# Seven-product matmul for one more batch of a fused attention and MLP-mixer kernel, with three weight sums moved

## The chip, the cores and the metric

The kernel runs on one core of one Trainium2 chip. The metric is the device time of one execution in microseconds (us). PE is TensorE, PEld its weight loads, DVE VectorE, ACT ScalarE, POOL GpSimd, SP SyncE, which issues most of the DMAs.

## The reference

Eight batches of a linear attention with cosine weights (8 heads, 576 rows, head width 64) feed an MLP mixer: a token part, then a channel part of two matmuls (512 to 1536 to 512). Cut to what matters:

```python
q_p, k_p = phi(q), phi(k)              # relu, times cos and sin of the position
kv  = einsum('bhsf,bhsd->bhfd', k_p, v)
x   = einsum('bhsf,bhfd->bhsd', q_p, kv) / den     # 8 x 576 x 512 in all
h   = maximum(x.T @ w_tok1, 0) @ w_tok2
u   = x + h.T
h2  = maximum(u @ w_ch1, 0) @ w_ch2    # the second channel matmul
out = u + h2
```

## The kernel before

A batch has 576 rows: 512 are worked on as four tiles of 128 rows, and the last 64 of two batches share one tile. These tail tiles of all eight batches are kept (`u_tail`) and go through the channel part together at the very end, as a ninth pass.

Each batch passes through the same steps. `feat` makes q and k features on ACT or DVE (its last letter: A or D; P is POOL), `cast` turns v to bf16, `turnx` transposes q features by DMA from SP's queue into `qpT`. `kvm` and `kvo` form and copy kv. `numf` and `numfo` form the numerator and divide it on DVE. `mix` and `mixo` are the first token matmul with relu, `um` the second. `uo` (DVE) adds x, `ubc` (POOL) casts to bf16, `utx` transposes the result by DMA into `uT`. `up` and `upo` are the first channel matmul and its relu into `h1` (12 blocks of 128 channels by 512 rows). The second channel matmul has two forms. In the plain one, `dn` adds 12 matmuls of 128x512 for each of four row tiles (`dnw` and `dnj` are orders of it), and `o` adds u on DVE and stores. In the other, `channel7`, h1 and `w_ch2` are split in two by two blocks, and seven products of block sums (Winograd's form of Strassen's method) take the place of eight: each product is 12 matmuls of 128x256. `p1` to `p7` are the products with the sums that follow them, `s_part` and `s3` make sums of h1 blocks on DVE, and `quad_weights` makes sums of blocks of `w_ch2`: t1 (in place of one block), t2, t3 and t4.

All instructions are in an order written by hand, on each engine in program order. The string `PLAN` (lines 18 to 57) lists the first part word by word: all of batches 0 and 1 through their channel parts, the attention of batch 2 and the features of batch 3. Both batches use the plain form of the second channel matmul there. From line 837 a loop runs p = 2 to 7: `channel7` does the channel part of batch p (lines 664 to 736), and after each of its slots calls hooks (`hooks7`) that issue attention of batch p + 1, features of batch p + 2 and loads of p + 3. For p = 2 alone, hooks in slots 0 and 8 also issue the four weight sums. Each product of `channel7` shares one of four PSUM buffers (`psM`) with the first matmul's `c_ps`: p1 and p2 use one bank after the other, p5 and p3 too, so that ACT must have copied p1's result (`va`) before p2, and p5's (`vc`) before p3. p7's bank is the one that p2's sum frees. At the end `channel7` runs once more for the tail rows, with `fine=True`: other order of products, p4 in two halves, and stores after each part, from the queues of SP and ACT.

Of the kernel before, what the change touches and what calls it, by code (L numbers as in the profile page):

```python
# [9 lines left out]
F32 = mybir.dt.float32  # L10
# [5 lines left out]
QUADS = 2  # L16
# [29 lines left out]
cast.2.0.1.2.P kvm.2.2 kvo.2.2.A turnx.2.4.1 ld.3.k.2.wd6 o.0.3 up.1.0 upo.1.0.A up.1.9 numf.2.3 numfo.2.3  # L46
up.1.4 upo.1.9.A numf.2.1 up.1.2 numfo.2.1 upo.1.4.A o.0.1 up.1.5 numf.2.0 upo.1.5.A upo.1.2.A numfo.2.0
feat.3.q.3.2.0.A feat.3.q.1.2.0.A feat.3.q.2.2.0.D ld.3.v.2.v22 cast.3.4.1.2.P up.1.10 up.1.3 numf.2.2
mix.2.0.2 numfo.2.2 upo.1.10.D up.1.8 up.1.6 numf.2.4 feat.3.q.2.2.1.A upo.1.8.D mix.2.1.2 mix.2.2.2 up.1.1
numfo.2.4 feat.3.q.1.2.1.A mix.2.3.2 mix.2.4.2 mixo.2.2.A feat.3.q.3.2.1.D upo.1.3.D turnx.3.2.2  # L50
feat.3.q.4.2.1.D upo.1.1.D up.1.7 feat.3.q.0.2.0.A upo.1.6.A up.1.11 feat.3.k.2.2.0.D feat.3.q.4.2.0.D
feat.3.k.4.2.1.A turnx.3.4.1 feat.3.q.0.2.1.D upo.1.11.A um.2.1 um.2.0 feat.3.k.0.2.1.D upo.1.7.A
cast.3.1.1.2.P uo.2.1 ubc.2.1 uo.2.0 dnj.1.3.0 dnj.1.3.1 cast.3.3.1.2.D turnx.3.0.2 feat.3.k.0.2.0.A ubc.2.0
utx.2.1 dnj.1.0.0 utx.2.0 ld.4.q.2 dnj.1.2.0 tb.1 feat.3.k.4.2.0.A dnj.1.2.1 cast.3.0.1.2.D o.1.2
feat.3.k.1.2.0.A cast.3.2.1.2.P feat.3.k.2.2.1.D ld.4.v.2.k22 dnj.1.1.0 dnj.1.1.1 ld.4.k.2.k32 feat.3.k.3.2.1.A
dnj.1.0.1 feat.3.k.3.2.0.A feat.3.k.1.2.1.A o.1.0 o.1.3 tm.2 to.2 o.1.1
# [3 lines left out]
def kernel(  # L60
# [11 lines left out]
    nc = tc.nc  # L72
# [194 lines left out]
    def relu(eng, dst, src):  # L267
        if eng == "A":
            nc.scalar.activation(dst, src, AF.Relu)  # L269
        else:  # L270
            nc.vector.tensor_relu(dst, src)  # L271

    class Batch:
# [261 lines left out]

        def o(self, j):
            nc.vector.tensor_add(self.u[:, j, :], self.ps.pop(("o", j)), self.u[:, j, :])
            if j % 2:
                for p_ in range(2):
                    nc.sync.dma_start(out=out_rows(self.b, p_, j - 1, 2), in_=self.u[p_::2, j - 1:j + 1, :])  # L540
# [36 lines left out]
    def channel(uT, u, store, by_slot, hooks, fine=False):  # L577
        h1 = one.tile([P, NCH, 4 * P], BF16, name="h1")
        slot = 0
# [7 lines left out]
        for mi in range(NCH):  # L587
            c_ps = psM.tile([P, 512], F32, name="c_ps", tag="psM")
            for ki in range(NCC):
                nc.tensor.matmul(c_ps, wc1[:, ki, mi * P:(mi + 1) * P], uT[:, :, ki, :],  # L590
                                 start=(ki == 0), stop=(ki == NCC - 1))
            relu(by_slot[mi], h1[:, mi, :], c_ps)
            step()
        for j in range(4):
            if fine and j == 3:
                for cs in (slice(0, Dm // 2), slice(Dm // 2, Dm)):
                    o_ps = psM.tile([P, Dm // 2], F32, name="o_ps", tag="psM")
                    for ki in range(NCH):
                        nc.tensor.matmul(o_ps, h1[:, ki, j * P:(j + 1) * P], wc2[:, ki, cs],
                                         start=(ki == 0), stop=(ki == NCH - 1))  # L600
                    nc.vector.tensor_add(u[:, j, cs], o_ps, u[:, j, cs])
                    store(j, u, cs)
                break
            o_ps = psM.tile([P, Dm], F32, name="o_ps", tag="psM")
            for half in range(2):
                for ki in range(half * NCH // 2, (half + 1) * NCH // 2):
                    nc.tensor.matmul(o_ps, h1[:, ki, j * P:(j + 1) * P], wc2[:, ki, :],
                                     start=(ki == 0), stop=(ki == NCH - 1))
                if half:
                    nc.vector.tensor_add(u[:, j, :], o_ps, u[:, j, :])  # L610
                    store(j, u)
                step()

    K2, D2 = NCH // 2, Dm // 2
    t2, t3, t4 = (const.tile([P, K2, D2], BF16, name=f"t{i}") for i in (2, 3, 4))

    def quad(a, b):
        return wc2[:, a * K2:(a + 1) * K2, b * D2:(b + 1) * D2]

    t1 = quad(0, 1)  # L620

    def quad_weights():
        return [lambda: nc.vector.tensor_sub(t3, quad(1, 1), quad(0, 1)),
                lambda: nc.vector.tensor_sub(t1, quad(0, 1), quad(0, 0)),
                lambda: nc.gpsimd.tensor_sub(t2, quad(1, 1), t1),
                lambda: nc.vector.tensor_sub(t4, quad(1, 0), t2)]

    def channel7(uT, u, store, by_slot, hooks, fine=False):
        h1 = one.tile([P, NCH, 4 * P], BF16, name="h1")
        slot = 0  # L630

        def step():
            nonlocal slot
            for f in hooks.get(slot, ()):
                f()
            slot += 1

        def tok(a, b):
            return h1[:, a * K2:(a + 1) * K2, b * 2 * P:(b + 1) * 2 * P]

        a11, a12, a21, a22 = tok(0, 0), tok(1, 0), tok(0, 1), tok(1, 1)
        s1 = one.tile([P, K2, 2 * P], BF16, name="s1")
        s2 = one.tile([P, K2, 2 * P], BF16, name="s2")
        va = w2r.rearrange("p n s -> p (n s)").bitcast(F32)[:, :2 * D2].rearrange("p (a b) -> p a b", a=2)
        vb = one.tile([P, 2, D2], F32, name="vb")
        vc = one.tile([P, 2, D2], F32, name="vc")
        u11, u12 = u[:, 0:2, :D2], u[:, 0:2, D2:]
        u21, u22 = u[:, 2:4, :D2], u[:, 2:4, D2:]

        def s_part(dst, f, a, b, n):  # L650
            ks = (slice(0, 4), slice(4, K2))[n]
            f(dst[:, ks], a[:, ks], b[:, ks])

        def product(ps, a, b, first, jjs=(0, 1)):
            for jj in jjs:
                for ki in range(K2):
                    nc.tensor.matmul(ps[jj] if isinstance(ps, list) else ps[:, jj], a[:, ki, jj * P:(jj + 1) * P], b[:, ki],  # L657
                                     start=(first and ki == 0 and (jj == 0 or isinstance(ps, list))), stop=ki == K2 - 1,
                                     skip_group_check=True)

        def bank():
            return psM.tile([P, 2, D2], F32, name="m_ps", tag="psM")

        for mi in range(NCH):
            c_ps = psM.tile([P, 512], F32, name="c_ps", tag="psM")
            for ki in range(NCC):
                nc.tensor.matmul(c_ps, wc1[:, ki, mi * P:(mi + 1) * P], uT[:, :, ki, :],  # L667
                                 start=(ki == 0), stop=(ki == NCC - 1))
            relu(by_slot[mi], h1[:, mi, :], c_ps)
            if mi == NCH - 2:  # L670
                s_part(s1, nc.vector.tensor_add, a21, a22, 0)
                s_part(s2, nc.vector.tensor_sub, s1, a11, 0)
            if mi == NCH - 1:
                s_part(s1, nc.vector.tensor_add, a21, a22, 1)
                s_part(s2, nc.vector.tensor_sub, s1, a11, 1)
            step()
        ps = {}

        def p1():
            ps["A"] = bank()  # L680
            product(ps["A"], a11, quad(0, 0), True)
            nc.scalar.copy(va, ps["A"])

        def p2():
            product(ps["A"], a12, quad(1, 0), False)
            nc.vector.tensor_add(u11, ps["A"], u11)
            if fine:
                store(0, u, 2, slice(0, D2))

        def p3():  # L690
            product(ps["C"], s1, quad(1, 1), False)
            nc.vector.tensor_add(u12, ps["C"], u12)
            store(0, u, 2, slice(D2, Dm) if fine else slice(0, Dm))

        def p4():
            if fine:
                E = [psA.tile([P, D2], F32, name="m2_ps", tag="psA") for _ in range(2)]
                for jj in range(2):
                    product(E, a22, t4, True, (jj,))
                    nc.vector.tensor_add(u21[:, jj], E[jj], u21[:, jj])  # L700
                store(2, u, 2, slice(0, D2))
            else:
                E = bank()
                product(E, a22, t4, True)
                nc.vector.tensor_add(u21, E, u21)

        def p5():
            ps["C"] = bank()
            product(ps["C"], s1, t1, True)
            nc.scalar.copy(vc, ps["C"])  # L710
            nc.vector.tensor_sub(s1, a12, s2)
            nc.gpsimd.tensor_add(u22, u22, vc)

        def p6():
            ps["B"] = bank()
            product(ps["B"], s2, t2, True)
            nc.vector.tensor_add(va, ps["B"], va)
            nc.vector.tensor_add(u12, u12, va)

        def p7():  # L720
# [158 lines left out]
```

## Time and profile before

| what | value |
|---|---|
| median of 9 runs | 266.87 us |
| lowest and highest | 266.16 and 544.47 us |
| profiled execution (one of the nine) | 544.47 us |
| span of its instructions | 542.7 us |
| mean clock of PE granted in it | 1.000 |
| DMA moved over its span | 53.41 MB, mean 98 GB/s |

The profiled execution is the long one of the nine; the other eight lie between 266.16 and 267.42 us. Durations of single instructions come from it. Busy times of the engines, the chain of work that ended last, and groups of equal instructions are read from it in the prediction. A group's line names the line of the kernel, the engine, the operation, what it writes and reads, its count, then busy time and mean of one, then the idle time before.

### The profile page before, as it was taken

How to read it: one execution, taken by the hardware profiler on the slowest of the kernel's cores; microseconds unless marked ns; L12 is line 12 of the kernel's file. 1: busy time of each engine (PE TensorE's matmuls, PEld its weight loads, DVE VectorE, ACT ScalarE, POOL GpSimd, SP SyncE). 2: the span in 40 equal slices, each digit the busy share in tenths (PEclk: the TensorE clock that was granted, in tenths of full speed). 3: DMA queues.
4: the chain of work that ended last, by engine and by line, in shares of the span. 5: the costliest groups of instructions: out<-in, count | busy, mean ns of one | idle time of the engine just before them, and what ended most of it. 6: DMA issues, size and time to landing. Idle time of an engine off the chain costs nothing.

```text
span 542.7 us, 5478 instructions
## 1 busy us (share of the span) xinstructions
PE 531.3 (98%) x2165; PEld 257.7 (47%) x2181; DVE 205.4 (38%) x374; ACT 142.1 (26%) x228; POOL 67.0 (12%) x82
## 2 busy tenths in 40 slices
PE   8999999999999999999999999999999999999996
PEld 3964354343334435543465346533654364364353
DVE  5253434444423334523442443344234334143143
ACT  5252161013410432243323332333411201111210
POOL 1530000200020401120121011301100111001010
DMA  8998200923584606480429034301510012001002
GB/s 281 216 250 229 62 27 1 228 82 126 97 206 152 207 0 120 142 294 18 90 47 317 22 60 76 89 0 34 103 79 0 11 29 87 0 1 77 0 1 79
DMA packets 79434, 53.41 MB, mean 98 GB/s; under 512 B 47792, under 2 KB 77232, under 8 KB 79408
## 3 DMA queue, kind: packets, MB, share of 16 engines
q1 hardware_dynamic: 74688, 48.77, 31.9%
q0 software_dynamic: 4144, 3.77, 4.5%
q10 hardware_dynamic: 576, 0.52, 0.3%
q8 instruction: 17, 0.28, 0.2%
q14 instruction: 9, 0.07, 0.0%
HBM read 35.85 MB, written 9.44 MB: 83 GB/s over the span
## 4 chain that ended last, share of the span: by engine, by line
PE 97%; DVE 1%; issue 1%
PE c_ps L667 29%; PE m_ps L657 25%; PE c L513 8%; PE o L525 8%; PE b L434 7%; PE u L461 6%; PE kv L362 4%; PE nf L391 3%; PE tr L312 2%; PE wm L193 2%; PE tr L346 2%; PE ut L489 1%; PE nm L391 1%; PE uT L451 1%; PE utr L481 0%
## 5 line engine op out<-in xcount | busy, mean ns | idle before, releaser
L667 PE MATMUL c_ps<-uT,wc 128*128 128x512 bf16 x288 | 144.2, 679 | 0.0
L269 ACT ACTIVATE h<-c_ps 128x512 bf16<-128x512 f32 x66 | 39.4, 597 | 209.0 <-PE c_ps L667 152.0
L667 PEld LDWEIGHTS <-wc 128*128 128x128 bf16 x336 | 46.7, 145 | 87.3 <-issue 87.1
L657 PEld LDWEIGHTS <-h 128*128 128x128 bf16 x336 | 50.5, 150 | 31.3 <-issue 4.4
L513 PE MATMUL c<-uT,wc 128*128 128x512 bf16 x96 | 47.5, 683 | 0.2 <-issue 0.2
L657 PEld LDWEIGHTS <-s 128*128 128x128 bf16 x252 | 37.1, 147 | 21.6
L525 PE MATMUL o<-wc,h 128*128 128x512 bf16 x92 | 45.0, 679 | 1.0 <-issue 1.0
L265 POOL CAST ub<-u 128x1024 bf16<-128x1024 f32 x14 | 14.9, 1062 | 229.5 <-DVE u L466 205.7
L271 DVE TENSOR_SCALAR h<-c_ps 128x512 bf16<-128x512 f32 x18 | 12.4, 692 | 79.0 <-PE c_ps L667 79.0
L657 PE MATMUL m_ps<-wc,h 128*128 128x256 bf16 x168 | 42.3, 448 | 0.0
L657 PE MATMUL m_ps<-t,h 128*128 128x256 bf16 x168 | 42.3, 451 | 0.0
L657 PE MATMUL m_ps<-wc,s 128*128 128x256 bf16 x168 | 42.1, 445 | 0.0
L434 PE MATMUL b<-x,w 128*128 128x512 bf16 (+1 forms) x84 | 39.5, 628 | 1.1 <-issue 1.1
L391 PEld LDWEIGHTS <-qpT 128*128 128x128 bf16 x320 | 25.1, 129 | 23.0 <-issue 19.4
L410 DVE TENSOR_SCALAR den<-nf 128x8 f32<-128x8 f32 x30 | 5.0, 166 | 71.9 <-PE nf L391 71.9
L461 PE MATMUL u<-B,w 128*128 128x512 bf16 x64 | 31.9, 681 | 0.0
L525 PEld LDWEIGHTS <-h 128*128 128x128 bf16 x96 | 14.0, 149 | 27.0 <-issue 27.0
L513 PEld LDWEIGHTS <-wc 128*128 128x128 bf16 x96 | 14.2, 152 | 25.1 <-issue 25.1
L466 DVE TENSOR_TENSOR u<-u,x 128x1024 f32<-128x1024 f32 x16 | 19.6, 1223 | 16.5 <-PE u L461 16.5
L331 ACT ACTIVATE qp<-qt,cos_t 128x512 bf16<-128x512 f32 x33 | 23.1, 712 | 3.8 <-DMA qt<-in_q_dram 3.8
L434 PEld LDWEIGHTS <-w 128*128 128x128 bf16 x90 | 13.2, 151 | 21.0 <-issue 18.4
L362 PEld LDWEIGHTS <-kp 128*128 128x128 bf16 x320 | 20.8, 129 | 4.5 <-issue 4.5
(117 smaller groups left out, 503.8 us busy)
## 6 DMA issues: line engine op xcount, KB each, us to landing
out_dram<-u SPq DMA_DIRECT2D x32, 256.0 KB, 2.4
qt<-in_q_dram SPq DMA_DIRECT2D x8, 640.0 KB, 7.6
kt<-in_k_dram SPq DMA_DIRECT2D x8, 640.0 KB, 6.5
qt<-in_q_dram SPq DMA_DIRECT2D x8, 512.0 KB, 6.3
kt<-in_k_dram SPq DMA_DIRECT2D x8, 512.0 KB, 5.4
vt<-in_v_dram SPq DMA_DIRECT2D x6, 640.0 KB, 6.4
vt<-in_v_dram SPq DMA_DIRECT2D x6, 512.0 KB, 5.3
wc<-in_moe_w_ch_dram POOLq DMA_DIRECT2D x4, 384.0 KB, 7.5
```

Source lines behind the costliest of these rows:

```text
L265: (nc.scalar.copy if eng == "A" else ENG[eng].tensor_copy)(dst, src)
L269: nc.scalar.activation(dst, src, AF.Relu)
L331: nc.scalar.activation(dst, src, AF.Relu, scale=tab)
L362: nc.tensor.matmul(ps[:, hh * (D + 1):(hh + 1) * (D + 1)], self.kp[:, j, h].rearrange("p f d -> p (f d)"), vbf[self.c][:, j, h, :D + 1], s ...
L391: nc.tensor.matmul(nm[:, hh * (D + 1):(hh + 1) * (D + 1)], self.qpT[:, j * H + h, :], self.kv[:, h, :D + 1], start=(not eps or hh == 0), s ...
L434: nc.tensor.matmul(b1[:, mi], w1[:, col(self.c, j), mi * P:(mi + 1) * P], self.x[:, j, cs], start=(j == 0 and (g == 2 or mi == 0)), stop=( ...
L461: nc.tensor.matmul(ps[:, jj], w2[:, ki, 1 + 2 * g + jj, :], self.B1[:, ki, :], start=(ki == 0), stop=(ki == NT - 1))
L466: nc.vector.tensor_add(self.sb("u")[:, js, :], self.ps.pop(("u", g)), self.x[:, js, :])
L513: nc.tensor.matmul(ps, wc1[:, ki, mi * P:(mi + 1) * P], self.uT[:, :, ki, :], start=(ki == 0), stop=(ki == NCC - 1))
L525: nc.tensor.matmul(self.ps["o", j], self.h1[:, ki, j * P:(j + 1) * P], wc2[:, ki, :], start=(ki == 0), stop=(ki == NCH - 1))
L657: nc.tensor.matmul(ps[jj] if isinstance(ps, list) else ps[:, jj], a[:, ki, jj * P:(jj + 1) * P], b[:, ki], start=(first and ki == 0 and (j ...
L667: nc.tensor.matmul(c_ps, wc1[:, ki, mi * P:(mi + 1) * P], uT[:, :, ki, :], start=(ki == 0), stop=(ki == NCC - 1))
```

## The change

Batch 1's second channel matmul takes the seven-product form too. Its products and sums (`m.1.…`) stand in the plan in place of the `dnj` and `o` words. The weight sums move from the hooks of p = 2 into the plan (`tq`): t3 from DVE to POOL, t2 stays on POOL, t1 and t4 stay on DVE. Eight features and casts around them go to other engines. `channel7` becomes the class `Seven` with the same steps, and the plain `channel`, unused since p starts at 2, is removed. In the hooks one q feature goes from slot 5 to slot 7. In the tail pass the sum of u21 and vb goes from POOL (in p7) to DVE (in p3).

```diff
-QUADS = 2
@@ PLAN, from the attention of batch 2 on
-cast.2.0.1.2.P kvm.2.2 kvo.2.2.A turnx.2.4.1 ld.3.k.2.wd6 o.0.3 up.1.0 upo.1.0.A up.1.9 numf.2.3 numfo.2.3
+cast.2.0.1.2.P tq.3.P kvm.2.2 kvo.2.2.A turnx.2.4.1 ld.3.k.2.wd6 o.0.3 up.1.0 upo.1.0.A up.1.9 numf.2.3 numfo.2.3
 up.1.4 upo.1.9.A numf.2.1 up.1.2 numfo.2.1 upo.1.4.A o.0.1 up.1.5 numf.2.0 upo.1.5.A upo.1.2.A numfo.2.0
-feat.3.q.3.2.0.A feat.3.q.1.2.0.A feat.3.q.2.2.0.D ld.3.v.2.v22 cast.3.4.1.2.P up.1.10 up.1.3 numf.2.2
+feat.3.q.3.2.0.A feat.3.q.1.2.0.A tq.1.D tq.2.P feat.3.q.2.2.0.A ld.3.v.2.v22 cast.3.4.1.2.P up.1.10 up.1.3 numf.2.2
 mix.2.0.2 numfo.2.2 upo.1.10.D up.1.8 up.1.6 numf.2.4 feat.3.q.2.2.1.A upo.1.8.D mix.2.1.2 mix.2.2.2 up.1.1
-numfo.2.4 feat.3.q.1.2.1.A mix.2.3.2 mix.2.4.2 mixo.2.2.A feat.3.q.3.2.1.D upo.1.3.D turnx.3.2.2
-feat.3.q.4.2.1.D upo.1.1.D up.1.7 feat.3.q.0.2.0.A upo.1.6.A up.1.11 feat.3.k.2.2.0.D feat.3.q.4.2.0.D
-feat.3.k.4.2.1.A turnx.3.4.1 feat.3.q.0.2.1.D upo.1.11.A um.2.1 um.2.0 feat.3.k.0.2.1.D upo.1.7.A
-cast.3.1.1.2.P uo.2.1 ubc.2.1 uo.2.0 dnj.1.3.0 dnj.1.3.1 cast.3.3.1.2.D turnx.3.0.2 feat.3.k.0.2.0.A ubc.2.0
-utx.2.1 dnj.1.0.0 utx.2.0 ld.4.q.2 dnj.1.2.0 tb.1 feat.3.k.4.2.0.A dnj.1.2.1 cast.3.0.1.2.D o.1.2
-feat.3.k.1.2.0.A cast.3.2.1.2.P feat.3.k.2.2.1.D ld.4.v.2.k22 dnj.1.1.0 dnj.1.1.1 ld.4.k.2.k32 feat.3.k.3.2.1.A
-dnj.1.0.1 feat.3.k.3.2.0.A feat.3.k.1.2.1.A o.1.0 o.1.3 tm.2 to.2 o.1.1
+numfo.2.4 feat.3.q.1.2.1.A mix.2.3.2 mix.2.4.2 mixo.2.2.A feat.3.q.3.2.1.A upo.1.3.D tq.4.D m.1.sums.2.5 turnx.3.2.2
+feat.3.q.4.2.1.D upo.1.1.D up.1.7 feat.3.q.0.2.0.A upo.1.6.A up.1.11 upo.1.7.A upo.1.11.A feat.3.k.2.2.0.D
+feat.3.q.4.2.0.A feat.3.q.0.2.1.A turnx.3.4.1 um.2.1 um.2.0 m.1.p1 feat.3.k.4.2.1.A cast.3.1.1.2.P uo.2.1 ubc.2.1 uo.2.0
+ubc.2.0 utx.2.1 m.1.sums.0.2 feat.3.k.0.2.1.A m.1.sums.5.6 m.1.s3 turnx.3.0.2 utx.2.0 ld.4.q.2 tb.1
+cast.3.0.1.2.A m.1.p4 feat.3.k.0.2.0.A feat.3.k.4.2.0.A cast.3.3.1.2.P m.1.p2 cast.3.2.1.2.P feat.3.k.1.2.0.A
+ld.4.v.2.k22 m.1.p5 ld.4.k.2.k32 feat.3.k.2.2.1.A m.1.p6 feat.3.k.3.2.1.A feat.3.k.3.2.0.A feat.3.k.1.2.1.A
+m.1.p7 m.1.p3 tm.2 to.2
@@ the weight sums
+    def tq(i, eng):
+        dst, a, b = {3: (t3, quad(1, 1), quad(0, 1)), 1: (t1, quad(0, 1), quad(0, 0)),
+                     2: (t2, quad(1, 1), t1), 4: (t4, quad(1, 0), t2)}[i]
+        ENG[eng].tensor_sub(dst, a, b)
@@ the class Seven, from channel7 (p1, p2, p4, p5, p6, s3 with the same steps)
+        def sums(self, a, b):
+            ks = slice(a, b)
+            nc.vector.tensor_add(self.s1[:, ks], self.a21[:, ks], self.a22[:, ks])
+            nc.vector.tensor_sub(self.s2[:, ks], self.s1[:, ks], self.a11[:, ks])
...
+        def p3(self):
+            self.product(self.ps["C"], self.s1, quad(1, 1), False)
+            nc.vector.tensor_add(self.u12, self.ps["C"], self.u12)
+            if self.fine:
+                self.store(0, self.u, 2, slice(D2, Dm))
+                nc.vector.tensor_add(self.u21, self.u21, self.vb)
+            else:
+                self.store(0, self.u, 2)
...
+        def p7(self):
+            self.product(self.bank("D"), self.a21, t3, True)
+            nc.vector.tensor_add(self.vb, self.ps["D"], self.va)
+            if not self.fine:
+                nc.gpsimd.tensor_add(self.u21, self.u21, self.vb)
+            nc.vector.tensor_add(self.u22, self.u22, self.vb)
+            self.store(2, self.u, 2, slice(D2, Dm) if self.fine else slice(0, Dm))
@@ class Batch
+        def m(self, f, *a):
+            if not hasattr(self, "seven"):
+                self.seven = Seven(self.h1, self.u, store_batch(self.b))
+            getattr(self.seven, f)(*a)
@@ hooks
-            for i, slot in enumerate((1, 2, 3, 4, 5, 7, 9, 10, 11, 12)):
+            for i, slot in enumerate((1, 2, 3, 4, 7, 7, 9, 10, 11, 12)):
                 at(slot, m.feat, "q", i // 2, 2, i % 2, "A")
-        if quads:
-            for f, slot in zip(quad_weights(), (0, 0, 0, 8)):
-                at(slot, f)
```

## The prediction

> **What bounds the kernel now.** I read the head of the page first, for who is busy, then the chain of waits, for what the end hangs on.
>
> ```profile
> span 542.7 us, 5478 instructions
> PE 531.3 (98%) x2165; PEld 257.7 (47%) x2181; DVE 205.4 (38%) x374; ACT 142.1 (26%) x228; POOL 67.0 (12%) x82
> PE 97%; DVE 1%; issue 1%
> ```
>
> PE is busy for 98% of the span and is 97% of the chain. But this execution took 544.47 us, and the other eight shown took 266.16 to 267.42 (the median of all nine is 266.87). Its PE went at about half the pace of theirs, though the clock beside it is 1.000. DVE, ACT, POOL and DMA need not follow PE's pace, so cover measured here is only about half as deep in the median run. I therefore make each sum twice: against 544.47, and with PE at the faster pace.
>
> The end of the same chain, in order of time, has the price of the change (start, us, what, count):
>
> ```profile
> 454.12 22.43 PE c_ps L667 x48
> 476.55 19.54 PE m_ps L657 x84
> ```
>
> 48 matmuls of 512 columns, in a row and unbroken, take 22.43 us, 467 ns each. 84 of 256 columns take 19.54 us, 233 ns each. A matmul costs its columns here; the weight load of each lies beside it. The grouped lines (busy time, mean of one) show what PE drops and what comes instead:
>
> ```profile
> L525 PE MATMUL o<-wc,h 128*128 128x512 bf16 x92 | 45.0, 679 | 1.0 <-issue 1.0
> L711 DVE TENSOR_TENSOR s<-h,s 128x1536 bf16<-128x1536 bf16 x7 | 6.7, 958 | 15.4 <-PE m_ps L657 15.4
> L718 DVE TENSOR_TENSOR u<-u,w2r 128x512 f32<-128x512 f32 x6 | 4.2, 692 | 0.2
> L725 DVE TENSOR_TENSOR u<-u,vb 128x512 f32<-128x512 f32 x6 | 10.7, 1786 | 0.6
> L724 POOL TENSOR_TENSOR u<-u,vb 128x512 f32<-128x512 f32 x6 | 7.6, 1263 | 26.0 <-DVE vb L723 26.0
> L625 POOL TENSOR_TENSOR t<-wc 128x1536 bf16<-128x1536 bf16 x1 | 3.1, 3087 | 23.2 <-DVE wc L624 23.2
> ```
>
> L718 and L725 are the same sum in form, yet L725 takes 1.09 us more: it runs beside POOL's L724. The stretch of the change, by windows (length, then busy time and count of PE, PEld, DVE, ACT, POOL):
>
> ```profile
> 132.00:146.00 14.00, 13.86 (x37) 4.79 (x37) 6.70 (x14) 2.73 (x4) 1.17 (x2) 1.00 0.36 70
> 146.00:172.00 26.00, 25.84 (x56) 8.25 (x56) 5.04 (x6) 4.74 (x8) 3.51 (x4) 1.00 0.66 175
> ```
>
> From 146 on (um, then the 48 matmuls of dnj) DVE has 5.04 us of work in 26. There is room, even in half of it.
>
> [...]
>
> **The change part by part.**
>
> (1) PE: dnj and o of batch 1 become p1 to p7. Removed are 48 matmuls x 467 ns = 22.4 us, added 84 x 233 = 19.5: -2.9 us on the chain, against 544.47. For the median: by the ratio of the runs (2.04) -1.42[...]. I take -1.3. Bounds: -1.45 above. [...]
>
> (2) The block sums tq leave the stage of p = 2 (DVE three x 0.95, POOL one x 3.09) for the plan: tq.1 and tq.4 on DVE, tq.2 and tq.3 on POOL (6.2 us). For tq.3 POOL has some 6 us of PE work (kvm.2, five up, three numf at the estimated pace) before tq.1. [...] DVE's next work (numfo.2, upo.10, upo.8, numfo.4) reads PSUM, one SBUF input at most. tq.4 waits for tq.2; what would queue behind it is sums, feat and upo.1, and so p1. From tq.1 to tq.4 there are five up, two numf and ten mix matmuls, 7.0 us of PE at the estimated pace: hidden. The relief in p = 2 is off the chain: 0, at most -0.5.
>
> (3) New DVE work: sums 2.55 us, s3 0.95, s1 for p3 0.96, five sums with a bank 3.45, u12 0.69, u22 1.79 = 10.4, less four o (2.74) and six feats and two casts moved to ACT and POOL (4.1): some 5.5 us more with tq.1 and tq.4. A walk at the faster pace, 0 where numf.2.4 ends. PE: eight mix and three up to 4.3, um to 6.05, then products of 1.31: p1 to 7.4, p4 8.7, p2 10.0, p5 11.3, p6 12.6, p7 13.9, p3 15.2, tm 15.65. DVE: numfo 1.06, upo.3 1.75, tq.4 2.7, sums.2.5 3.8, feat 4.3, upo.1 5.0, feat 5.45, uo 6.7 and 7.9; then sums.0.2 waits for POOL's ubc.2.0 (1.06) [...] and ends at 9.85, sums.5.6 10.4, s3 11.4, p4's sum 12.1, p2's 12.8. p5 finds its blocks in order; p7 wants the bank that p2's sum frees, from 12.6: late by 0.2. The new s1 is there at 13.75 for p3. I take +0.3 for stalls of this kind; bounds 0 and +1.5.
>
> (4) ACT gains six feats (0.71; 0.62 apart where they follow each other), a cast and two copies, some 5.4 us. In the walk p1's copy ends near 8.0 (p2 writes that bank from 8.7), vc's near 12.1 (p3 from 13.9), and the last k feature of batch 3 at about 14.6, with kvm.3 at 16.5. 1.9 us of cover; nothing counted. If it goes, each us late is a us of PE.
>
> (5) uT of batch 2 for the first c_ps: uo 7.9, ubc 9.0. On SP's queue utx.2.1 (1.25 us), turnx.3.0.2 (about 2) and utx.2.0 (1.25) now follow in this order, so utx.2.0 is issued at about 11 and lands 3.1 to 3.8 us later, by 14.6. Needed at 15.65: 1 us of cover, nothing counted. POOL's casts and the stores of batch 1 that go behind have more.
>
> (6) The tail. POOL's sum u21 + vb goes; DVE does it after p3. In the profiled execution DVE waits for PE before each of the last sums:
>
> ```profile
> 535.44 0.69 DVE L686 TENSOR_TENSOR u_tail<-m_ps,u_tail 128x512 f32<-128x512 f32 x1 [2.13 <-PE m_ps L657]
> 538.21 0.42 DVE L700 TENSOR_TENSOR u_tail<-m_ps,u_tail 128x256 f32<-128x256 f32 x1 [0.95 <-PE m_ps L657]
> ```
>
> so there it saves 0. At the faster pace, 0 at p7's end: before, vb 0.7, u22 2.6 (1.79), p3's 3.3, p2's 4.0, p4's halves 4.4 and 4.85, with PE done at 3.93. After: u22 1.4 (0.69), p3's 2.1, the moved sum 2.8, p2's 3.5, halves 3.95 and 4.4. -0.4; bounds 0 and -0.5. p5's sum stays on POOL.
>
> Sum: against 544.47, -2.9 = 541.6. For the median -1.3 + 0.3 - 0.4 = -1.4: 265.5.
>
> **Rivals.**
> (a) PE's gain is eaten in part: 256-column products dearer than the estimate, or p7 and the first c_ps short of their inputs by some tenths. For it: the walk's small margins. Against it: two for one in the trace's pitches (467, 233). Time 266.4 to 267.1.
> (b) Slower: DVE's queue becomes the bound from um to p7. Place: p2's sum, which frees the bank of p7. It is 0.2 us late already, so from there each us more is one us of PE. Every POOL cast that meets one of sums, s3 or tq.4 costs up to 1.06, every late feat 0.5, and p4's and p2's sums stand behind them all. At 1.4 us more than I took the gain is gone, at 2 us it is slower; with three such meetings (3 us) 268.5. For it: DVE has some 5.5 us more to do where PE has 1.2 less. Against it: 5.04 us busy of 26 in the window.
> (c) More gain: the sums taken out of p = 2 stood in the way at the faster pace, and the tail gives its most: 264.2.
> That the change doesn't do what it says I don't see: the 48 dnj matmuls leave the plan, and the blocks are summed after batch 0's last matmul with w_ch2.
>
> **How the numbers follow.** A measurement of this kernel tells about 0.2% (0.53 us) from none. Forecast, 264.6 to 266.3: 0.55. (a) 0.22, half of it within 0.2%. (b) 0.18. (c) 0.05. Faster 0.55 + 0.05 + 0.09 = 0.69, same 0.13, slower 0.18. The range: 264.4 leaves out (c), 267.8 holds (a) and the beginning of (b), so under 0.2 is left out. The forecast's own range is 264.6 to 266.3.
>
> **What would show it.** In the profile after: L525's count down by 48 (less what records miss) and a block of 84 m_ps of about 19.6 us after um; no PE idle before p5, p7 or the first c_ps; the tail's moved sum at 0.69 and L725's last at 0.69 instead of 1.79. It is wrong if PE idles before a product for DVE or ACT, or if the 256-column block gives less in the median than in the profile.

## The result, and the profile after

The changed kernel takes 269.27 us (median of 11 runs, 267.14 to 271.17), the kernel before 266.86 beside it (33 runs). The ratio is 1.0089, with a 95% interval of 1.0071 to 1.0107: slower by 0.9%, about 2.4 us, where 265.5 and a gain were forecast. The ratio leaves out the long execution of the kernel before (544.47) and the longest of the changed kernel (271.17), which count as slow.

The profiled execution took 268.27 us. Here PE ran at the pace that the prediction had only estimated. The head of the page, and the chain's shares by engine; then the same two of the kernel before, from a later profile (c_before, below) that ran at this pace too:

```profile
span 266.5 us, 5564 instructions
PE 253.7 (95%) x2201; PEld 164.6 (62%) x2217; DVE 211.6 (79%) x377; ACT 144.9 (54%) x237; POOL 74.4 (28%) x85
PE 69%; DMA 12%; DVE 11%; issue 4%; POOL 1%; SPq 1%; ACT 0%; DVEq 0%; POOLq 0%
```

```profile
PE 254.7 (96%) x2181; PEld 161.3 (61%) x2181; DVE 204.7 (77%) x374; ACT 139.3 (53%) x228; POOL 68.8 (26%) x82
PE 88%; DVE 4%; DMA 4%; issue 1%; ACT 1%; DVEq 0%; ACTq 0%
```

At this pace PE is 88% of the chain before the change and 69% after it, and DMA and DVE together go from 8% to 23%. DVE's busy share hardly moves, 77% and 79%; the 38% in the prediction is about the same work (205.4 us there, 204.7 in c_before) over a span twice as long.

The last two blocks on the chain (start, us, what, count) and the groups of the products and of the sum with vb (busy time and mean):

```profile
222.81 10.36 PE c_ps L710 x48
233.17 9.17 PE m_ps L330 x84
```

```profile
L330 PE MATMUL m_ps<-wc,s 128*128 128x256 bf16 x192 | 23.6, 273 | 0.4 <-DVE s L371 0.4
L639 PE MATMUL o<-wc,h 128*128 128x512 bf16 x45 | 11.2, 379 | 0.2
L384 DVE TENSOR_TENSOR u<-u,vb 128x512 f32<-128x512 f32 x7 | 12.5, 1787 | 0.7
L384 DVE TENSOR_TENSOR u_tail<-u_tail,vb 128x512 f32<-128x512 f32 x1 | 0.7, 693 | 0.1
```

48 matmuls of 512 columns take 10.36 us and 84 of 256 columns 9.17: 215.8 and 109.2 ns each, so 1.31 us a product. The prediction's walk used this price as the author's estimate; no trace had shown it then. o's count fell from 92 to 45 (some records are missing in each trace), and the tail's sum from 1.79 to 0.69 us. So the parts that were to bring time are there. The time went somewhere else, in batch 2's features, before the first product. PE, then DVE, then POOL of the changed kernel in order of time (start, us, engine, line, what; in brackets the idle time before it):

```profile
58.40 1.67 PE L639 MATMUL o<-wc,h 128*128 128x512 bf16 x7
62.31 0.59 PE L603 MATMUL ut<-B,w 128*128 128x512 bf16 x2 [2.24 <-DVE uT L264]
```

```profile
57.60 4.06 DVE L447 TENSOR_SCALAR kp<-kt,cos_t 128x512 bf16<-128x512 f32 x2
61.58 1.27 DVE L264 COPY uT<-utr 128x1024 bf16<-128x1024 bf16 x2
```

```profile
58.12 3.25 POOL L301 TENSOR_TENSOR t<-wc 128x1536 bf16<-128x1536 bf16 x1
```

The POOL line is `tq.3`. Two k features on DVE, 0.48 us each by themselves, take 4.06 us together. The first, 0.83 us, begins beside POOL's cast just before; the second, 3.31 us, stands beside `tq.3`. The copies of uT stand behind them on DVE, and PE has nothing to do for 2.24 us.

### The profile page after: what moved, and what is told of

It reads as the page before. It is cut to its first block, busy times and chain, and to the rows that moved or that the text cites. A ratio compares the mean times of both kernels' runs of the same rounds, so it can differ in the third digit from the quotient of the medians.

```text
span 266.5 us, 5564 instructions
## 1 busy us (share of the span) xinstructions
PE 253.7 (95%) x2201; PEld 164.6 (62%) x2217; DVE 211.6 (79%) x377; ACT 144.9 (54%) x237; POOL 74.4 (28%) x85
## 4 chain that ended last, share of the span: by engine, by line
PE 69%; DMA 12%; DVE 11%; issue 4%; POOL 1%; SPq 1%; ACT 0%; DVEq 0%; POOLq 0%
PE c_ps L710 27%; PE m_ps L330 21%; PE b L548 5%; DMA qt<-in_q_dram 4%; PE c L627 4%; PE kv L476 3%; DMA wc<-in_moe_w_ch_dram 3%; PE nf L505 3%; PE u L575 3%; DMA uT<-ub 2%; DVE kp L447 2%; DMA kt<-in_k_dram 2%; DVE u L580 2%; PE o L639 1%; SPq L143 1%
## 5 line engine op out<-in xcount | busy, mean ns | idle before, releaser
L710 PE MATMUL c_ps<-uT,wc 128*128 128x512 bf16 x288 | 70.5, 379 | 0.3 <-DMA uT<-ub 0.2
L710 PEld LDWEIGHTS <-wc 128*128 128x128 bf16 x336 | 30.7, 97 | 33.2 <-issue 1.2
L330 PEld LDWEIGHTS <-h 128*128 128x128 bf16 x384 | 37.5, 98 | 6.1
L264 POOL CAST vbf<-vt 128x512 bf16<-128x512 f32 (+3 forms) x29 | 18.9, 688 | 28.3 <-DMA vt<-in_v_dram 27.9
L330 PE MATMUL m_ps<-wc,h 128*128 128x256 bf16 x192 | 23.6, 273 | 0.0
L330 PE MATMUL m_ps<-t,h 128*128 128x256 bf16 x192 | 23.6, 273 | 0.0
L627 PE MATMUL c<-uT,wc 128*128 128x512 bf16 x96 | 22.8, 379 | 0.1
L445 ACT ACTIVATE qp<-qt,sin_t 128x512 bf16<-128x512 f32 x32 | 22.8, 721 | 0.0
L528 DVE TENSOR_TENSOR x<-nf,den 128x512 bf16<-128x512 f32 x30 | 20.7, 691 | 1.0
L548 PE MATMUL b<-x,w 128*128 128x512 bf16 (+1 forms) x84 | 19.8, 354 | 0.3
```

The lines of the kernel that those rows point to most:

```text
L264: (nc.scalar.copy if eng == "A" else ENG[eng].tensor_copy)(dst, src)
L445: nc.scalar.activation(dst, src, AF.Relu, scale=tab)
L528: nc.vector.tensor_mul(dst, nmv[:, :, :, :D], den_b)
L548: nc.tensor.matmul(b1[:, mi], w1[:, col(self.c, j), mi * P:(mi + 1) * P], self.x[:, j, cs], start=(j == 0 and (g == 2 or mi == 0)), stop=( ...
L627: nc.tensor.matmul(ps, wc1[:, ki, mi * P:(mi + 1) * P], self.uT[:, :, ki, :], start=(ki == 0), stop=(ki == NCC - 1))
```

## The experiments

Two theories at first. P: t3 on POOL lengthens the DVE feature beside it (3.31 us instead of 0.48), and that is the loss. Q, the prediction's rival (b): DVE's queue between um and p3 is the loss. Later two more: D, that a later stage, waiting for a transposed tile, takes a gain back; and H, that the idle time itself costs clock. `tq.3` is the plan's word for t3's sum. Each ratio is against executions of the kernel before taken beside it, whose medians lay between 266.65 and 266.90.

| kernel | edit | median us (runs) | ratio to before, 95% |
|---|---|---|---|
| after | the change | 269.27 (11) | 1.0089 (1.0071 to 1.0107) |
| c_before | none | 266.76 (1) | single run |
| x_tq3_dve | after, t3 on DVE | 267.19 (22) | 1.0019 (1.0005 to 1.0032) |
| y_before_tq3 | before, t3 early on POOL | 270.61 (6) | 1.0120 (1.0086 to 1.0155) |
| z_split3 | after, t3 in three instructions | 268.78 (6) | 1.0076 (1.0060 to 1.0091) |
| t_before_tail | before, the tail's part alone | 266.24 (22) | 0.9979 (0.9966 to 0.9993) |
| y_fill | y_before_tq3, PE busy in the wait | 269.33 (6) | 1.0102 (1.0084 to 1.0120) |
| w3_casts_later | x_tq3_dve, three POOL casts later | 267.45 (14) | 1.0013 (0.9990 to 1.0036) |
| w4_v_later | w3_casts_later, one v load later | 265.67 (7) | 0.9957 (0.9941 to 0.9974) |
| b_v_later | before, that v load later | 266.47 (14) | 0.9995 (0.9986 to 1.0004) |
| w5_utx_first | w4_v_later, uT's second transpose ahead of a q transpose | 265.60 (10) | 0.9956 (0.9939 to 0.9973) |

**The kernel before, at the pace of its median.**

> The kernel before, unchanged, for a profile at the pace of its median. Theory P [...]: in it the feature feat.2.k.4.2.0 on DVE takes 0.48 us, not 3.3, and PE does not idle between the last dnw matmuls of batch 0 and tm.1, so PE idle there is below 0.5 us where after had 2.2. Theory Q (DVE's queue behind um): PE idles here as much as in after, and the difference of the two kernels lies between um and the first c_ps. Time near 266.9 us in both.

The same places of its profile, PE and then DVE:

```profile
60.15 0.59 PE L489 MATMUL ut<-B,w 128*128 128x512 bf16 x2
```

```profile
58.20 0.87 DVE L333 TENSOR_SCALAR kp<-kt,cos_t 128x512 bf16<-128x512 f32 x2
58.98 1.28 DVE L265 COPY uT<-utr 128x1024 bf16<-128x1024 bf16 x2
```

The same two features take 0.87 us, the copies start 2.6 us earlier, and PE goes on without a gap. As P has it.

**t3 alone, taken away and put in.** In the changed kernel t3 goes to DVE; in the kernel before it goes to POOL, at the place where the change has it.

```diff
-cast.2.0.1.2.P tq.3.P kvm.2.2 ...
+cast.2.0.1.2.P kvm.2.2 ...
-... tq.1.D tq.2.P ...
+... tq.3.D tq.1.D tq.2.P ...
```

> The changed kernel with one of the four weight sums, t3, taken from GpSimd back to VectorE, just before t1. Theory P: the loss comes from GpSimd's t3 (3.25 us) [...] while a k feature of batch 2 waits on DVE; without it the idle of 2.2 us at tm.1 goes and the time falls from 269.3 to 265.5 to 266.5 us, below the kernel before. Theory Q: the loss comes from DVE's queue between um and p3 of batch 1; DVE gets 0.95 us more, so the time stays at 269 us or rises to 270. Theory C (a lower granted clock under more load): stays near 269 us.

```diff
-cast.2.0.1.2.P kvm.2.2 ...
+cast.2.0.1.2.P tq3 kvm.2.2 ...
@@ quad_weights, slots (0, 0, 8)
-        return [lambda: nc.vector.tensor_sub(t3, quad(1, 1), quad(0, 1)),
-                lambda: nc.vector.tensor_sub(t1, quad(0, 1), quad(0, 0)),
+        return [lambda: nc.vector.tensor_sub(t1, quad(0, 1), quad(0, 0)),
@@ OPS
+           "tq3": lambda: nc.gpsimd.tensor_sub(t3, quad(1, 1), quad(0, 1))}
```

> The kernel before with nothing changed but t3: on GpSimd, at the place in the plan where the changed kernel has it, instead of on DVE in the hooks of p = 2. Theory P: this alone costs 2.2 to 2.8 us, 269.1 to 269.7 us. Theories Q and C: no product, sum or matmul is added, so 266.5 to 267.1 us.

Put into the kernel before, with not one product added, t3 on POOL costs 3.8 us (2.3 to 4.1 by the interval), where P had 2.2 to 2.8. Taken out of the changed kernel, it gives some 2 us back, but the time ends at 267.2, not at 265.5 to 266.5. So P is the cause of the loss, Q as the main cause falls, and two questions come up: why t3 costs more in the median than the idle time, and what holds back the gain once it is gone.

**Why it costs more than the idle time.** The windows of y_before_tq3 (length, then busy time and count of PE, PEld, DVE, ACT, POOL, then the granted clock of PE):

```profile
56.00:62.40 6.40, 4.19 (x32) 2.27 (x30) 6.40 (x7) 1.76 (x3) 5.10 (x3) 1.00 1.04 216
62.40:66.00 3.60, 3.57 (x44) 2.58 (x44) 3.56 (x7) 0.48 (x1) 0.00 (x0) 0.55 1.16 279
66.00:70.00 4.00, 4.00 (x33) 2.08 (x32) 2.74 (x8) 1.91 (x4) 0.00 (x0) 0.98 1.09 361
```

PE idled for 2.24 us up to 62.43, and right after it its clock is 0.55 for 3.6 us: some 1.6 us are lost after the wait is over. Not every execution does this. Of the six of y_before_tq3, four had a mean clock of 0.991 to 0.993 and took 270.5 to 270.9 us, two had 0.998 or 0.999 and took 268.2 and 268.9. To test it, PE was given work for just that wait:

```diff
-dnw.0.10 dnw.0.11
+dnw.0.10 fill.0.10 dnw.0.11
+        def fill(self, n):
+            for _ in range(n):
+                nc.tensor.matmul(self.ps["o", 0], zero[:, :P], zero, start=False, stop=False)
```

> As y_before_tq3, and ten matmuls of 128x512 with a zero operand added to an accumulator of batch 0 before its last twelve-row step, so that PE works through the 2.2 us in which it idled. The time that PE waits for is the same. Theory H (an idle of 2.2 us makes the granted clock of PE fall for a while, in some executions): the clock stays at 0.995 or more in all runs, and the median falls from 270.6 to 268.2 to 268.9 us, the time of the runs without such a fall. Rival (the longer runs have another cause): 270.6 us or more again.

All six runs had a clock of 0.995 or more and took 268.5 to 269.6; the long ones were gone. The median lies 0.4 us above what H named. It is 1.3 us below that of y_before_tq3, but the intervals of the two ratios overlap; what speaks for H is the clock, which was low in four of six executions and then in none of six. The changed kernel may lose time in the same way, but no trace of such an execution was kept: its own profile has the same 2.24 us of idle and a clock of 1.00 after it. Of its twelve recorded executions five had a mean clock of 0.992 to 0.994 and took 269.7 to 271.2 us, seven had 0.997 or more and took 267.1 to 269.3. A mean of 0.994 alone says little: two executions of b_v_later had it at 266.2 and 266.8 us.

**t3 in three instructions.**

```diff
-        ENG[eng].tensor_sub(dst, a, b)
+        for k in ((0, 2), (2, 4), (4, 6)) if i == 3 else ((0, K2),):
+            ENG[eng].tensor_sub(dst[:, slice(*k)], a[:, slice(*k)], b[:, slice(*k)])
```

> The changed kernel with t3's sum on GpSimd at the same place, in three instructions of 128x512 instead of one of 128x1536. Theory P: [...] the k feature on DVE gets in after the first, takes about 1.3 us instead of 3.3 and the time falls by 1 to 2 us, to 267.3 to 268.3. [...] Theories Q and C: 269 us as before.

DVE's two features at this place take 2.66 us together instead of 4.06, PE's idle time falls from 2.24 to 1.20 us, no execution has a clock below 0.998. Each feature takes 1.37 us, and both end at 60.81, before POOL's third piece does (61.83). What makes a feature longer beside POOL these lengths don't show. But the median fell by only 0.5 us where 1 to 2 were expected, and the two intervals overlap. PE's wait for uT at batch 4's first c_ps is 0.91 us here, where the changed kernel's trace has 0.24. That was the first sign of D.

**Where the gain went once t3 was away.** When PE begins at five places, in us, from one profile each; the last two columns are the stretches from um to kvm of batch 3 (the products lie in it) and from there to kvm of batch 5. Not every profiled execution lies at its kernel's median: that of the changed kernel took 268.27 us (median 269.27), x_tq3_dve's 266.27 (267.19), w5_utx_first's 266.81 (265.60). A few tenths between rows say little.

| kernel | kvm 2 | um 2 | kvm 3 | kvm 5 | last product | um 2 to kvm 3 | kvm 3 to kvm 5 |
|---|---|---|---|---|---|---|---|
| c_before | 60.58 | 75.64 | 89.02 | 141.81 | 258.34 | 13.38 | 52.79 |
| after | 63.00 | 78.13 | 91.12 | 144.31 | 260.40 | 12.99 | 53.19 |
| x_tq3_dve | 60.34 | 75.64 | 88.68 | 142.22 | 258.31 | 13.04 | 53.54 |
| w3_casts_later | 60.40 | 75.69 | 88.66 | 143.39 | 259.49 | 12.97 | 54.73 |
| w4_v_later | 60.45 | 75.74 | 88.82 | 141.61 | 257.73 | 13.08 | 52.79 |
| w5_utx_first | 61.97 | 77.26 | 89.45 | 142.43 | 258.82 | 12.19 | 52.98 |

The changed kernel is 2.4 us late at kvm 2, all of it t3. Of the 1.19 us that the products save, 0.4 arrive at kvm 3. DVE of the changed kernel between um and p3, four of the five sums that are longer than by themselves (s2, s1, s3 and the new s1, 0.43, 0.29, 0.95 and 0.96 us by themselves; the second s2, 0.58 instead of 0.29, is the fifth), and POOL's sum of u21 and vc:

```profile
82.05 1.14 DVE L322 TENSOR_TENSOR s<-s,h 128x512 bf16<-128x512 bf16 x1
83.12 0.69 DVE L321 TENSOR_TENSOR s<-h 128x256 bf16<-128x256 bf16 x1
...
84.35 1.36 DVE L325 TENSOR_TENSOR h<-h 128x1536 bf16<-128x1536 bf16 x1
...
86.83 1.40 DVE L371 TENSOR_TENSOR s<-h,s 128x1536 bf16<-128x1536 bf16 x1
```

```profile
86.14 1.27 POOL L372 TENSOR_TENSOR u<-u,vc 128x512 f32<-128x512 f32 x1 [1.24 <-ACT vc L370]
```

They have two inputs in SBUF. POOL's casts ran beside the first three, and its own sum beside the new s1; p3, which needs the new s1, began 0.57 us after p7's end. The casts were then issued later. A first form of this, w1_pool_later, and w2_v_later built on it, put cast.3.3 and cast.3.2 behind ld.4.v, so that two of batch 3's casts took batch 4's v: part of the computation was changed. They took 277.08 and 275.97 us and say nothing on the question.

> The changed kernel with t3 on VectorE and with three GpSimd casts (tb.1, cast.3.3, cast.3.2) issued after p5's sum instead of before it. Theory P: the block sums between um and p3 on DVE are stretched by some 1.8 us by GpSimd's casts (1.14, 0.69, 1.36 and 1.23 us in the trace where 0.43, 0.29, 0.95 and 0.96 are their own length), and so p3 waits; with the casts later s3 and the new s1 fall to about 0.95 each, PE doesn't idle before p7 and p3, and the time falls by 0.4 to 0.6 us, to 266.6 to 266.8. Theory D (a later stage takes the gain back: the first c_ps of batch 4 waits for uT, whose DMA took 6.6 us beside the loads): the stage of batch 1 ends earlier, the wait at batch 4 grows by as much, and the time stays at 267.2.

> As w1_pool_later, and the v load of batch 6 issued in slot 16 instead of slot 9, behind the transposes of batch 4. Theory D: the two uT transposes land in 3 to 4 us instead of 6.7, the wait of 0.6 us or more at batch 4's first c_ps goes, and the time falls to 265.6 to 266.2, below the kernel before. If nothing but the sums on DVE held the gain back, it is the same as w1_pool_later.

In the next form the load stands behind the casts:

```diff
-... m.1.s3 turnx.3.0.2 utx.2.0 ld.4.q.2 tb.1
+... m.1.s3 turnx.3.0.2 utx.2.0 ld.4.q.2
-... cast.3.3.1.2.P m.1.p2 cast.3.2.1.2.P feat.3.k.1.2.0.A
-ld.4.v.2.k22 m.1.p5 ld.4.k.2.k32 ...
-m.1.p7 m.1.p3 tm.2 to.2
+... m.1.p2 feat.3.k.1.2.0.A
+m.1.p5 cast.3.3.1.2.P cast.3.2.1.2.P ld.4.v.2.k22 ld.4.k.2.k32 ...
+m.1.p7 m.1.p3 tm.2 to.2 tb.1
```

> The changed kernel with t3 on VectorE, the two GpSimd casts cast.3.3 and cast.3.2 issued after p5's sum, ld.4.v after them, and tb.1 at the end of the plan. Theory P: the block sums between um and p3 on DVE are stretched by some 1.8 us by GpSimd's casts; with the casts later the second s2, s1, s3 and the new s1 take less than 0.5, 0.5, 1.0 and 1.0 us, PE doesn't idle before p7 and p3, and the time falls by 0.4 to 0.6 us, to 266.6 to 266.8. Theory D (a later stage takes the gain back, the first c_ps of batch 4 waiting for uT): the stage of batch 1 ends earlier, the wait at batch 4 grows by as much, and the time stays at 267.2.

DVE of w3_casts_later, three of the four sums, and PE's two waits that are left:

```profile
81.14 0.28 DVE L321 TENSOR_TENSOR s<-h 128x256 bf16<-128x256 bf16 x1
...
81.67 0.95 DVE L325 TENSOR_TENSOR h<-h 128x1536 bf16<-128x1536 bf16 x1
...
83.73 0.95 DVE L371 TENSOR_TENSOR s<-h,s 128x1536 bf16<-128x1536 bf16 x1
```

```profile
87.80 1.02 PE L710 MATMUL c_ps<-uT,wc 128*128 128x512 bf16 x4 [0.61 <-DMA uT<-ub]
142.53 1.02 PE L710 MATMUL c_ps<-uT,wc 128*128 128x512 bf16 x4 [1.79 <-DMA uT<-ub]
```

These sums are short again (the first s1 and s2 still meet ubc.2.0, at 0.74 and 1.14 us). The new s1 now begins together with POOL's sum, and it is POOL's that is longer, 2.09 us instead of 1.27. The seven products run without a gap. But the time is 267.45, no better than x_tq3_dve: the gain that P expected of the sums did not come through. What was a wait for s1 is now a wait of 0.61 us for uT at batch 2's first c_ps, and kvm 3 begins no earlier than in x_tq3_dve (88.66 and 88.68). The wait at batch 4 is 1.79 us, where x_tq3_dve's profile has 0.59. That D named the place is borne out. Its reason, that batch 1's stage ends earlier, is not what this trace shows: PE comes to batch 4's wait at about the same time in both (140.2), and uT lands later, its second transpose issued at 135.6 instead of 134.5.

The second wait lies beside a v load that is issued just ahead of the transposes. Landing times of batch 4's two uT transposes (from issue, us), first in w3_casts_later, then with the v load of batch 6 moved behind them:

```profile
DMA to landing us min/median/max: 6.8/6.9/7.0
```

```profile
DMA to landing us min/median/max: 3.3/3.4/3.4
```

```diff
-            at(16 if nxt == 5 else 9, load, nxt, "v")
+            at(16 if nxt in (5, 6) else 9, load, nxt, "v")
```

> As w3_casts_later, and the v load of batch 6 issued in slot 16 instead of slot 9, behind the transposes of batch 4. Theory D: the two uT transposes land in 3 to 4 us instead of 6.7, the wait at batch 4's first c_ps goes, and the time falls to 265.6 to 266.2, below the kernel before. If nothing but the sums on DVE held the gain back, it is the same as w3_casts_later.

> The kernel before, and only the v load of batch 6 in slot 16 instead of slot 9. Theory D: here PE does not wait for uT (no such wait in its trace), so the move gains nothing: 266.5 to 267.1 us, and the gain of w4_v_later is the changed kernel's own, which that wait had hidden. Rival: the load's place is worth the same in any kernel; then 265.6 to 266.0 us.

265.67 us, faster than the kernel before by 0.43% (0.26 to 0.59). Its interval lies below that of w3_casts_later. The same move in the kernel before changes nothing that can be told (b_v_later): it had no such wait, though its transposes took 5.2 to 6.2 us to land there (c_before). So the load's place is worth nothing by itself; it lets a gain through. How much of that gain is the seven products' stays open. The tail's part alone gives 0.21% (below), which leaves about 0.6 us of their 1.19 by difference, and the move of the load without that of the casts was not run.

```diff
-... m.1.s3 turnx.3.0.2 utx.2.0 ld.4.q.2
+... m.1.s3 utx.2.0 turnx.3.0.2 ld.4.q.2
```

> As w4_v_later, and utx.2.0 ahead of turnx.3.0.2 on SP's queue. The prediction's step 5 took the order utx, turnx, utx as covered; in w3 and w4 PE waits 0.6 and 0.7 us for uT at batch 2's first c_ps. If the queue's order is what is late, the wait goes and the time falls by 0.5 to 0.7 us, to 265.0 to 265.2; if the transfer itself is slowed by the loads beside it, it stays at 265.7.

In w5_utx_first's profile the wait at batch 2's first c_ps is gone, and from um to kvm 3 PE takes 12.19 us, 1.19 less than in the kernel before: the whole saving. The two transposes land in 3.3 to 4.0 us, about as in w4_v_later (3.5 to 4.1), but the second is issued 6.3 us after um began instead of 8.6. The median, 265.60, can't be told from that of w4_v_later, where 265.0 to 265.2 was expected. The profile of w5_utx_first began its first transposes after 1.2 us of idle on PE for a q feature, in a part that all these kernels share; the runs spread by 1.8 us, which hides half a microsecond. So in these two traces the order of the queue was late there and not the transfer, and what it is worth in the median stays open.

**The tail alone.**

```diff
             nc.vector.tensor_add(u12, ps["C"], u12)
             store(0, u, 2, slice(D2, Dm) if fine else slice(0, Dm))
+            if fine:
+                nc.vector.tensor_add(u21, u21, vb)
...
-            nc.gpsimd.tensor_add(u21, u21, vb)
+            if not fine:
+                nc.gpsimd.tensor_add(u21, u21, vb)
```

> The kernel before with only the tail's part of the change: in the last pass the sum of u21 and vb on VectorE after p3 instead of on GpSimd in p7. The prediction's step 6: the last sums end 0.4 us earlier, 266.4 us. Rival: in the profile of before at its median's pace the last two half sums run without a wait on PE of more than 0.1 us, but the stores end the execution in either case, so 0 to 0.2 us.

0.21% less (0.07 to 0.34), about 0.6 us by the ratio. That fits the prediction's 0.4; the rival's 0 to 0.2 lies at the edge of the interval. In the profiles little of it is where step 6 put it. From the start of PE's last product to the end of the last sum it is 2.11 us in c_before and 1.93 in t_before_tail, and from there to the end of the span 4.55 and 4.06. Before, the first stores go out 0.3 us after the last product began, behind the sum of 1.79 us, and then follow each other closely, the last one issued 1.2 us after the last sum. With that sum at 0.69 us they begin 0.8 us ahead of the last product, and the last is issued 0.7 us after the last sum.

## Why the prediction was wrong, point by point

**Step 2 is the one that failed**, at "For tq.3 POOL has some 6 us of PE work ... before tq.1". It asked when t3 is needed, and there no wait came. It did not ask what runs beside it. It looked at DVE's work beside tq.2, having read the price of such a meeting from L725 (1786 ns beside POOL, L718 692), and not beside tq.3, a subtraction of the same size (3.10 and 3.25 us). POOL's queue has nothing to wait for there, so t3 starts right behind cast.2.0, at 58.12, while DVE is still at batch 2's last k feature. In place of "hidden" stand 2.24 us of idle PE, and, in y_before_tq3's trace, a further 1.6 us of clock; t3 alone cost the kernel before 3.8 us.

Beside tq.2 the prediction was right. DVE's work there reads PSUM and kept its length (0.69 us is also the mean of all 30 of the first kind in this trace):

```profile
71.70 3.10 POOL L301 TENSOR_TENSOR t<-wc 128x1536 bf16<-128x1536 bf16 x1 [10.32 <-DVE wc L301]
72.04 0.69 DVE L528 TENSOR_TENSOR x<-nf,den 128x512 bf16<-128x512 f32 x1
72.65 1.28 DVE L270 TENSOR_SCALAR h<-c 128x512 bf16<-128x512 f32 x2
```

But its test, one input in SBUF at most, would have let tq.3 through: the k feature reads one tensor in SBUF, scaled by a column, and took 2.8 us longer all the same (3.31 instead of 0.48). By what means POOL's sum lengthened it was not shown, nor was t3 tried on POOL at a later place, such as that of tq.2.

**Step 1**: the matmuls that go and those that come measure 10.36 and 9.17 us, 1.19 saved, where the step took 1.3, the author's estimate, and the ratio of the runs gave 1.42. What was wrong is that this gain was carried to the end of the sum as if all of it arrived.

**Step 3** took 0.3 us for stalls of the products; 0.57 were measured at p3. The cause was the one named, POOL's work beside DVE's sums, but the walk counted one such meeting, at 1.06 us, and the trace shows five, of 0.29 to 0.71 us each, the one that delayed p3 with POOL's sum and not with a cast.

**Step 4**: no PE wait on ACT in the plan's stage of the changed kernel's trace.

**Step 5** claimed 1 us of cover for uT. There was none: with t3 and the casts out of the way PE waits 0.6 to 0.7 us for it (w3_casts_later, w4_v_later). It had utx.2.0 issued 6.7 us after um began; w4_v_later's trace has 8.6, and utx.2.1 alone kept the queue for 2.06 us instead of 1.25. In the changed kernel p3's delay hid most of that. And batch 4's uT, which no step looked at because nothing in it was changed, took back 0.24 to 1.79 us. At half the pace of PE in the profile shown before, no such wait can be seen; the prediction said that cover is thinner at the faster pace, but looked only at the stage of the change.

**Step 6** had the size: 0.4 us forecast, 0.6 by the ratio of t_before_tail (0.2 to 0.9). The reason was right only in part, and so it had some luck: the last sum ends some 0.2 us earlier in the profiles, and the stores, which it did not price, give the larger part.

Of the rivals, (b) had the side and the cause, DVE's work longer beside POOL's, but the wrong place: PE waits for no sum up to p7 and 0.57 us at p3, not 3. (a) was there besides: the gain was eaten in part. A meeting of DVE and POOL was priced at up to 1.06 us, three of them at 268.5, which the range to 267.8 left out; the one that came, with 3.25 us of POOL's work, made a feature 2.8 us longer.

From profile to profile the sum is now: t3 +2.4 us at kvm 2, +0.1 up to um 2, products and their waits -0.4 up to kvm 3, +0.4 up to kvm 5, -0.4 up to the last product (its cause was not looked for), the tail -0.6: 1.5 us, the difference of the spans (265.0 and 266.5). The medians differ by 2.4; the executions with a lower mean clock may account for part of the rest.

## What to carry to other kernels

Before a long instruction is given to GpSimd, list everything VectorE does while it can run, with one tensor in SBUF (here 2.8 us longer) or two (here 0.3 to 1.1), from the moment when it may start and not from the place where its result is due: t3 had nothing to wait for and began at 58.12, where t1, before which it was due, began at 70.67. A gain on the bound engine is only there at the end if every later wait that ran just in time moves as well; look for the transfers that landed barely ahead of their use, also in stages that the change doesn't touch. And a profile in which the bound engine runs at half its usual pace shows prices (DVE's work 205.4 us, at the usual pace 204.7), not cover (467 ns a matmul of 512 columns, at the usual pace 215.8).

## What the runs showed of the hardware

- In y_before_tq3's trace 2.24 us without a matmul were followed by 3.6 us at a mean granted clock of 0.55; in the changed kernel's trace the same 2.24 us were followed by a clock of 1.00. Four of six executions of y_before_tq3 had a mean clock of 0.991 to 0.993; with the wait filled by matmuls on zeros (y_fill), none of six was below 0.995.
- A DVE tensor_scalar from one float32 SBUF tensor to bf16 (0.48 us) took 3.3 us beside one POOL subtraction of 3.25 us (the changed kernel). With that subtraction in three instructions (z_split3) it took 1.37 us. DVE instructions that read PSUM kept their length beside a POOL subtraction of 3.10 us (0.69 us; the changed kernel).
- Where a DVE sum and a POOL sum began within 0.01 us of each other (w3_casts_later), DVE's kept its 0.95 us and POOL's took 2.09 instead of 1.27.
- Two DMA transposes of uT landed after 6.8 to 7.0 us behind a v load (w3_casts_later; 5.9 to 6.7 in x_tq3_dve, 5.2 to 6.2 in c_before) and after 3.3 to 3.4 us ahead of it (w4_v_later; 4.2 to 5.5 in w5_utx_first).
